# Forty columns for both score tiles, and another order of TensorE's work, in a two-layer recurrent attention kernel

## The chip, the core and the metric

The kernel runs on one core of a Trainium2 chip. The metric is the device time of one execution in microseconds. Before the change three runs gave 2647.1, 2651.34 and 2651.9 us; the median is 2651.34 us.

## What is computed

Two blocks, each applied twice with the same weights, with a residual around each. Block A is attention over segments of 32 rows with 8 memory rows; the output of the memory rows becomes the memory of the next segment, so the 64 segments are a recurrence. Block B is a gated feed-forward. All data are bf16.

```python
# x: (1, 2048, 576); 32 heads of 128; 8 memory rows; segments of 32 rows
def A(x, mem, Wq, Wk, Wv, Wo):
    for s in range(64):
        h = concat(mem, x[32*s : 32*s+32])          # 40 rows
        q, k, v = h @ Wq, h @ Wk, h @ Wv             # per head
        p = softmax(where(mask, q @ k.T * 128**-0.5, -1e9))   # 40 x 40 per head
        o = (p @ v) summed over heads through Wo
        mem = o[:8]; out.append(o[8:])
def B(x): return (silu(x @ w1) * (x @ w3)) @ w2      # 576 -> 4608 -> 576
x = x + A(layernorm(x)); x = x + B(layernorm(x))     # first layer
x = x + A(layernorm(x)); x = x + B(layernorm(x))     # second layer
```

## The kernel before

The second layer runs 8 steps behind the first (`LAG`), so there are 72 steps. Steps 0 to 7 and 64 to 71 hold one layer; the 56 steps between hold one segment of each layer, side by side: 80 columns move through the weights of Q and K, 40 for each layer.

The work is a list of nodes made by `make_nodes` (from line 263 on). A TensorE node is one letter of an order written out by hand as strings: `FIRST`, then `FOUR` eleven times, then `LAST` (`FOUR` covers four steps). TensorE issues strictly in this order. `plan` walks through it with a price and a due time for each node, and from that chooses the order on ACT, DVE, POOL and the DMA queues, and which of ACT and DVE evicts a bank. The letters that matter here:

- Q and q: the projection to queries and keys of four heads (eight in a one-layer step); Q takes the 512 rows of the model dimension that fill the array, q the 64 left over, for queries and keys in two row tiles at once.
- S: the scores of a group of eight heads (`scores`, called 4 times in a step). T: the transpose of the weights p on TensorE, in one-layer steps only; two-layer steps use a DMA transpose from `PB` to `PTS` on SP's queue, behind and ahead of the loads of feed-forward weights.
- P: p times values. O and o: the output projection and its tail. V, v, X, x, G, g: the value projections.
- F, f, W, w: the feed-forward up (F, its tail f) and down, with `W13`, its tail and `W2C` loaded from HBM into two buffers each.
- p, n, a, b: transposes around the residuals and layer norms.

Each node has a mode of the array: "full", "row" (two tiles of 64 rows), "col" (two tiles of 64 columns), "c32" (four of 32), or mixtures. Where a node can take either of two modes, `plan` gives it that of its neighbours.

In a two-layer step the queries of the two layers are two column tiles of the array. The weights loaded are the queries, the keys move. The tile of the first kind takes 64 columns (`R64`), of which the last 24 are columns that no later operation uses; the second takes `QW` = 40. Their outputs are rows 0 to 63 and 64 to 103 of one PSUM bank. The softmax (`sm_add` and what follows) then runs over rows 0 to 103, and `sm_pb` takes from it rows 0 to 39 and 64 to 103.

Every matmul is issued by one helper (line 729, `mm`), every activation by line 732, every DVE operation by line 735, every SP DMA by line 738, except the transposes (line 1274). The program is fully unrolled.

Of the kernel before, what the change touches and what calls it, by code (L numbers as in the profile page):

```python
# [13 lines left out]
P = 128  # L14
R64 = 64
# [6 lines left out]
QW = SEG + MEM  # L22
# [45 lines left out]
def role(t):  # L68

    return (t - LAG) % 2  # L70
# [156 lines left out]
def ewh(*ns):  # L227
# [2 lines left out]


FIRST = (
    "maqqQQQqSSvxVTXTqPQPSXSOOTPooOoTxPOoQqQSqqqSQQSSvTTVPTPOPoOTOPooOoQqqQvSSVqQQSqSTTPPOOoToTPaPOOooQqvqqSQVSQTQSqx"
    "PTSOPXOTToPoPOOooQqqpvSQVSnqQFFTSfqfPTQFOSPWTFOPoffTOPFOoooWQqfqQSFSVvqfqQQFTTSWPPFSOOxffXToFPWoTfOPFOooFQfqfqQS"
    "VqqvSQQSWTFSPTFfPOTOoPfWTOPFOoooFQffqqQSWQSqVvTSFfQqfWFSTafPFPOToWPTOPOOooobQqqqpQQQxSnXFvqfVSFfqqQQFfqSQPWQqfOS"
    "FPXxWOooPffFFPOOooWQQQqqfqFSFqfqQQQSFqqqfQQWFggfSGSGPGPgfFOOoPWGgfOPFOoooWFqqfQQFSqfqQQQSFvfqqQVSqWqQQfPPSFfOOWP"
    "FOfoFPaooOoWQQqqqqQSQQbSqqqQGSgQqPQGggSPGGPgOOOoPooOoQqqvpQpQQnSqqVqnSQFffqFQQPQqqfSFSOPWwfFOooFPfOWPwfFOooFqqfq"
    "QQQSqqqQQQSWwFfGSFqqfgQQPwWgSGFPGgfOOPWgfGFOoPOoooaqqQQQQqqwFfSSVvQQqqfFWSPwFqfqQQPFSwfOWOFPffFOwWoPOoooFfqqqQQW"
    "SQQqqqQSbQGSgqqQPQGSgOPGggOPGwOoPooOo"
)  # L240
FOUR = (
    "QqqqppQQvVSnnQFqfqqQQSFSFfqfqQQwWPFfPOOSWFoPowffFFPOOoowWQQfqfqFSFfqqqQQwQWSFgfqqQGQPQqgfSWSGFPOwoGggGPOPOOoooaF"
    "qfqqQQQSFqqqfQQQwWvSSVFPQFffqqQOPSWwoffFOPFOwPWOoooFqfqqQQWQSQqqqQQSwSbQQqgqgGSGPGPOoggGPOPOOooo"
)
LAST = (
    "QqqqppQQQqSvVSnnQQqqfFSqqQPQFSffOPFOwPWFOfFoPoofOoWQQQqqqwSQFQqqfGSqgQQPQqfSFGgqgPGSWwfFOFPOfgGOwoPOoooqqqQQQQqS"
    "WFfSVvqfqQFQQPWSwFqfqfQPFOSwWOPFffFOWwoPOoooFqqfqQQQSQFQqqfqQSVSvqqQQWwfSPFVvPWOwPOOobPooxOoXqpQpQqqvVSnSnQFFSTf"
    "fqPTQFSwFPWOTTffPOPOOooooFqffqQQSwFWSQvVqqQTSFPSTWPwFOTffTPOPOOoooowFWvxXVfqQQqfqSQSFFfqSQTwTSWPPFOffTOPFWTOFPwO"
    "ooooFfqfqQQSFSQwfqqQSWSVvTTFwWPffFPOTOTPWPOOoooowbqqpQQxvSSnXVFQfqqQTSTFfSPFPOwTOPFffooTOPFOoowQfqqqQSQSFvVTSQqf"
    "XPFSTwPOTffFPOTFPOOoooofxQfqqQSFSvVwTQqqFSffQwPTSFTPFPOffOTOPwOooooFQqQSqqvVSQQSqwTTSFPFPOoTOoTPffPOOoopfwfFFnFw"  # L250
    "fffFFFwffFFwfffFFwFwfffFFFwffFFwffFFwfffFFww"
)
ORDER = FIRST + FOUR * 11 + LAST
# [2 lines left out]
class Opt:  # L256

    qk, qkt, sc, tr, pv, wo, wog, vm = 0.0079, -0.0342, 0.0268, 0.1447, 0.0406, 0.2653, 0.0725, 0.1407
# [4 lines left out]
def make_nodes(em, nseg, pools, o=Opt, dma_bw=230e3, load_bw=380e3, tail_bw=330e3):  # L263
# [4 lines left out]
    def node(*a, **k):  # L268
        n = Node(*a, **k)
        n.prio += 1e-9 * len(nodes)  # L270
        nodes.append(n)
        return n

    def banks(n=2):
        return [Slot("bank") for _ in range(n)]
# [7 lines left out]
    def both(t):  # L283

        return len(layers_of(t - role(t))) == 2
# [104 lines left out]
    def step(t):  # L390
        ls = layers_of(t)
        nl = 2 if both(t) else 1
# [18 lines left out]
        for g, (h0, nh) in enumerate(GROUPS):  # L411
            qs, qe = [], []
            for uh, un in units(g, nl):
# [4 lines left out]
                if pre:  # L418
                    xl.append(node("DMA", 0.5, em.xq_load(t, uh, q), deps=[v[0] for v in [kept_qk.get((t // 4, uh // 4))] if v] + last_qk[-BACK:][:1], prio=pq - 0.3, acq=[q], lat=2.6, name="XL", ring=1.3))
                m_ = node("PE", 8 * un * mmq, em.qk(t, uh, un, b), deps=hx + hm[:1] + ([ld_h[g]] if t == 0 else []),  # L420
                          prio=pq, mode="full", acq=[q] + b, name="QK")
                last_qk.append(m_)
                n = node("PE", un * mmq, em.qk_tail(t, uh, un, b), deps=hx + hm + ([ld_h[g]] if t == 0 else []), prio=pq + o.qkt, mode="row",
                         acq=[q] + b, name="QKt")
                rd += [m_, n]
                me.setdefault(f"QK{g}", []).extend([m_, n])
                for r in (0, 1):
# [4 lines left out]
            s = banks(1)[0]  # L432
            sme = Slot("sme")
            pf = t + o.gstep * h0 / 8
            w40 = nh * QW
            sc = node("PE", nh * (0.0155 * nl if nl == 2 else 0.0255), em.scores(t, g, qs, s), deps=qe, prio=pf + o.sc, mode="col" if nl == 2 else "full/col",
                      acq=[s, sme], rel=[q for q, _, _ in qs], name="SC")
            a = node("DVE", dve(w40), em.sm_add(t, g, s, sme), deps=[sc], prio=pf, rel=[s], name="add")
            m_ = node("DVE", dve(w40, w40) + 0.13, em.sm_max(t, g, sme), deps=[a], prio=pf, name="maxsub")
# [14 lines left out]
            if paired(t):  # L454
                hn = [ht_ready[li, s] for s in (t + 1, t + 2) for li in (0, 1) if (li, s) in ht_ready]
                for blk in blks:
                    if blk // 2 not in vgs:
# [6 lines left out]
                      prio=pf + o.pv, mode="full/col", acq=b + ot, rel=[pts], name="PV")  # L464
# [21 lines left out]
        if nxt:  # L486
            m = 8 * len(nxt)
# [191 lines left out]
    for t in range(nst):  # L679
        if t % 4 == 2 and (t + 2) // 4 < ngrp:  # L680
            x_in((t + 2) // 4)
        if t == LAG:
            ht_mem[t].append(node("DVE", 0.1, em.init_mem(1, LAG), deps=[m0e] + reads_ht.get(LAG - R_HT, []), prio=LAG - 2, name="m0"))
        if role(t) == 0 or t == 0:
            vx_pair(t - role(t), t - 1 + o.vx)
        step(t)
        if t % 4 == 1 and t // 4 < ngrp:
            x_res(t // 4)
        if t % 4 == 3:
            job((t + 1) // 4 - 1)  # L690
        elif t == nst - 1:
            job(nst // 4)
# [12 lines left out]
class Emitter:  # L705
# [482 lines left out]
    def scores(self, t, g, qs, s):  # L1188

        def f(n):  # L1190
            nh = GROUPS[g][1]
            S = self.bk(s)[:, 0:nh * QW].rearrange("p (h k) -> p h k", h=nh)
            both = self.both(t)
            w = QW * self.nl(t)
            for i in range(max(un for _, _, un in qs)):
                for q, j0, un in qs:
                    if i >= un:
                        continue
                    Q = self.T.QKT[:, q.i]
                    for kd in ((0, 1) if both else (0,)):  # L1200
                        m = (R64 if kd == 0 else QW) if both else P if n.mode == "full" else QW
                        q0 = i * w + (QW * (kd ^ role(t)) if both else 0)
                        self.mm(S[64 * kd:64 * kd + m, j0 + i, :], Q[:, q0:q0 + m], Q[:, un * w + q0:un * w + q0 + QW],
                                True, True, **({"tile_position": (0, 64 * kd)} if n.mode == "col" else {}))
        return f
# [414 lines left out]
```

## Time and profile before

| | |
|---|---|
| median of 3 runs | 2651.34 us |
| span of the profiled execution | 2659.8 us (no time of its own beside the span is given) |
| TensorE: matmuls busy | 2571.8 us, 97% |
| TensorE: weight loads busy | 2214.4 us, 83% |
| DVE, ACT, POOL busy | 77%, 46%, 13% |
| `FIRST` | to 538.8 us |
| `FOUR`, eleven times | 538.8 to 2227.7 us |
| `LAST` | from 2227.7 us |

The profile is of one execution on the core. "PE" are matmuls, "PEld" weight loads, which overlap matmuls. A matmul's duration in the profile includes its way through the array; matmuls overlap, so what counts is the distance between starts. A row of the timeline gives start, length, engine, line, operation, tiles with shapes (the first shape of a merged group), and the count, with idle time ahead of it in brackets and what ended it. A row of waits gives who waited for whom: total us, times, longest. "issue" is idle time in which the engine waited for nothing that the profile shows.

### The profile page before, as it was taken

What the parts mean: (1) busy time and instruction counts of PE and PEld (TensorE: products, weight loads), DVE (VectorE), ACT (ScalarE), POOL (GpSimd) and SP (SyncE); (2) the same over time, 40 slices, a digit from 0 to 9 for tenths busy, and PEclk for the clock granted to TensorE, in tenths of its full rate; (3) what the DMA queues carried; (4) which work ended last, traced back from release to release, by engine and by line L of the source; (5) the groups of instructions that cost most, each with busy time, mean ns of one, the idle gap of its engine ahead of it and who ended that gap; (6) DMA issues with size and microseconds to landing.
All of it is one profiled execution on the core that took longest, in us unless ns stands there. A gap on an engine that the chain in (4) does not pass through costs nothing.

```text
span 2659.8 us, 132078 instructions
## 1 busy us (share of the span) xinstructions
PE 2571.8 (97%) x58776; PEld 2214.4 (83%) x58818; DVE 2045.3 (77%) x5137; ACT 1225.1 (46%) x3495; POOL 336.9 (13%) x399
## 2 busy tenths in 40 slices
PE   5899999999999999999999999999999999999998
PEld 4778887888888888888888888888888888888887
DVE  4777777777878778788777878877787788778876
ACT  2545453444545354454535444453544445344453
POOL 1111111011101111010111111011110111011110
PEclk8899999999999999999999999999999999999999
DMA  9045746565554655545465555546555554554457
GB/s 317 9 144 155 188 99 142 125 145 146 106 141 115 164 135 147 134 118 139 113 156 126 150 130 129 132 113 152 126 151 133 136 137 105 121 148 120 132 162 246
DMA packets 690428, 371.41 MB, mean 140 GB/s; under 512 B 234328, under 2 KB 682592, under 8 KB 689216
## 3 DMA queue, kind: packets, MB, share of 16 engines
q1 hardware_dynamic: 686320, 355.08, 52.6%
q8 instruction: 460, 7.54, 1.2%
q0 software_dynamic: 3024, 6.93, 1.0%
q10 hardware_dynamic: 512, 0.94, 0.1%
q14 instruction: 112, 0.92, 0.1%
HBM read 306.72 MB, written 2.36 MB: 116 GB/s over the span
## 4 chain that ended last, share of the span: by engine, by line
PE 85%; DMA 6%; DVE 5%; issue 1%; ACT 1%; SPq 0%; ACTq 0%; POOL 0%; DVEq 0%; POOLq 0%
PE bank L729 85%; DMA PTS<-PB 2%; DMA W<-in_B_w_dram 2%; DVE STAT L735 1%; DVE V L735 1%; DVE SME L735 1%; DVE PB L735 1%; DMA W<-in_A_Wq_dram 1%; DMA WO<-in_A_Wo_dram 0%; DMA W<-in_A_Wk_dram 0%; DVE HTT L735 0%; ACT V L732 0%; DVE XR L735 0%; DMA WV<-in_A_Wv_dram 0%; SPq L738 0%
## 5 line engine op out<-in xcount | busy, mean ns | idle before, releaser
L729 PEld LDWEIGHTS <-W 128*128 128x128 bf16 (+2 forms) x31872 | 1258.3, 100 | 150.0 <-issue 72.7
L729 PE MATMUL bank<-HT,W 128*128 128x80 bf16 (+3 forms) x23040 | 796.8, 197 | 23.6 <-issue 8.7
L729 PE MATMUL bank<-XTB,W 128*64 128x256 bf16 (+5 forms) x8832 | 667.4, 263 | 9.2 <-DMA W<-in_B_w_dram 5.8
L1264 POOL MEMSET PB<- 128x1024 bf16 x288 | 273.3, 953 | 1764.3 <-DMA PTS<-PB 1066.0
L732 ACT ACTIVATE QKT<-bank 128x128 bf16<-128x128 f32 (+2 forms) x1497 | 356.0, 316 | 276.9 <-PE bank L729 269.2
L729 PE MATMUL bank<-OT,WO 128*128 128x80 bf16 (+3 forms) x11520 | 414.3, 199 | 5.9 <-ACT OT L732 3.1
L729 PEld LDWEIGHTS <-WO 128*128 128x128 bf16 (+1 forms) x11520 | 385.9, 102 | 22.9 <-issue 10.8
L732 ACT ACTIVATE V<-bank 32x512 bf16<-32x512 f32 (+1 forms) x563 | 319.7, 585 | 174.5 <-PE bank L729 163.1
L729 PE MATMUL bank<-WV,HT 128*32 128x512 bf16 (+4 forms) x3735 | 366.0, 387 | 9.2 <-DMA WV<-in_A_Wv_dram 4.4
L729 PE MATMUL bank<-W2C,HTT 128*64 128x288 bf16 (+1 forms) x3136 | 317.2, 287 | 0.2 <-DMA W2C<-in_B_w_dram 0.2
L732 ACT ACTIVATE HTT<-bank 128x512 bf16<-128x512 f32 (+1 forms) x324 | 176.0, 550 | 277.9 <-PE bank L729 275.4
L735 DVE TENSOR_REDUCE STAT<-SME 104x8 f32<-104x320 f32 (+1 forms) x576 | 274.8, 477 | 29.9 <-ACT SME L732 20.3
L735 DVE TENSOR_TENSOR PB<-SME,STAT 40x128 bf16<-40x128 f32 (+4 forms) x912 | 275.3, 336 | 12.0 <-POOL PB L1264 1.0
L729 PEld LDWEIGHTS <-HT 128*32 128x32 bf16 (+5 forms) x3776 | 157.8, 101 | 139.6 <-issue 42.4
L735 DVE SCALAR_TENSOR_TENSOR HTT<-HTT,bank 128x512 bf16<-128x512 bf16 (+1 forms) x324 | 201.6, 622 | 82.3 <-ACT HTT L732 78.8
L732 ACT ACTIVATE SME<-SME 104x320 f32<-104x320 f32 (+1 forms) x288 | 135.5, 471 | 280.6 <-DVE SME L735 276.9
L729 PEld LDWEIGHTS <-HTT 128*64 128x64 bf16 (+1 forms) x3216 | 232.2, 105 | 32.6 <-issue 1.2
L735 DVE SCALAR_TENSOR_TENSOR XR<-bank,XR 128x288 f32<-128x288 f32 x574 | 240.6, 448 | 16.2 <-PE bank L729 11.8
L732 ACT ACTIVATE OT<-bank 128x320 bf16<-128x320 f32 (+2 forms) x430 | 164.1, 401 | 184.9 <-PE bank L729 171.9
L735 DVE CAST V<-bank 64x512 bf16<-64x512 f32 (+1 forms) x301 | 206.4, 686 | 43.4 <-PE bank L729 35.6
L735 DVE TENSOR_TENSOR HTT<-HTT,bank 128x512 bf16<-128x512 bf16 (+1 forms) x324 | 203.6, 628 | 28.1 <-PE bank L729 0.5
L735 DVE CAST QKT<-bank 128x192 bf16<-128x192 f32 (+4 forms) x423 | 124.4, 335 | 114.3 <-PE bank L729 111.3
(59 smaller groups left out, 1396.5 us busy)
## 6 DMA issues: line engine op xcount, KB each, us to landing
W<-in_B_w_dram SPq DMA_DIRECT2D x608, 256.0 KB, 3.7
W2C<-in_B_w_dram SPq DMA_DIRECT2D x304, 288.0 KB, 3.4
W<-in_B_w_dram SPq DMA_DIRECT2D x608, 32.0 KB, 3.3
W<-in_B_w_dram SPq DMA_DIRECT2D x16, 512.0 KB, 7.3
WO<-in_A_Wo_dram SPq DMA_DIRECT2D x4, 1152.0 KB, 9.8
XR<-in_A_x_dram POOLq DMA_DIRECT2D x16, 288.0 KB, 3.0
WV<-in_B_w_dram SPq DMA_DIRECT2D x8, 576.0 KB, 6.5
W<-in_A_Wq_dram SPq DMA_DIRECT2D x16, 256.0 KB, 7.1
```

The lines of the kernel that those rows point to most:

```text
L729: self.ch("PE", self.nc.tensor.matmul(out, lhsT=lhsT, rhs=rhs, start=start, stop=stop, skip_group_check=True, **k))
L732: self.ch("ACT", self.nc.scalar.activation(*a, **k))
L735: self.ch("DVE", getattr(self.nc.vector, fn_)(*a, **k))
L1264: return lambda n: self.ch("POOL", self.nc.gpsimd.memset(self.T.PB[:, pb.i, 0:GROUPS[g][1]], 0.0))
```

## The change

Three edits. In `scores` the first column tile loads `QW` = 40 columns too, so both tiles are alike. In `make_nodes` the price by which `plan` counts a score node of two layers falls from 0.0155 to 0.0126 us for each head and layer. And the three strings of the order are new: the same letters, each as often as before (709 in `FIRST`, 208 in `FOUR`, 604 in `LAST`), in another sequence, which was searched with a model of the instruction fetch for each 256 instructions.

```diff
 FIRST = (
-    "maqqQQQqSSvxVTXTqPQPSXSOOTPooOoTxPOoQqQSqqqSQQSSvTTVPTPOPoOTOPooOoQqqQvSSVqQQSqSTTPPOOoToTPaPOOooQqvqqSQVSQTQSqx"
...
+    "amqQqqSQQvSVTXxQSqTPPXTSPOoOOTPooOoQqQqvSSQqQSqSTxTVPTPOPTOPOOooooQqQSqVvSQqQQSTqPSTOPOTTPooPOOooaQqqqvSQVSqQTQST"
...
 FOUR = (
-    "QqqqppQQvVSnnQFqfqqQQSFSFfqfqQQwWPFfPOOSWFoPowffFFPOOoowWQQfqfqFSFfqqqQQwQWSFgfqqQGQPQqgfSWSGFPOwoGggGPOPOOoooaF"
-    "qfqqQQQSFqqqfQQQwWvSSVFPQFffqqQOPSWwoffFOPFOwPWOoooFqfqqQWQSQqqqQQSwSbQQqgqgGSGPGPOoggGPOPOOooo"
+    "QqqqppQQvVSnnQFqqfqQQSFSFfqfqQQPwFWPSffOFOwWoFffPFPOOoWoowQQqqqqQQFSSFqffqQQQQqfqgFSGWwPGSgfOPFGggoGPOPOOoowoFqq"
+    "fqQQWSQQQqqqfQwWSFSvVqfQPFOQqFSofPWwOPFffOFPWOowooFqqfqQQQSaWqqqQQQSwbSQQqgqGSGPgGPOggoGPOPOOooo"
 )
 LAST = (
-    "QqqqppQQQqSvVSnnQQqqfFSqqPQFSffOPFOwPWFOfFoPoofOoWQQQqqqwSQFQqqfGSqgQQPQqfSFGgqgPGSWwfFOFPOfgGOwoPOoooqqqQQQQqS"
...
+    "QQpqqqQQqSvpnSVqqQQnQqfSFfqFPQOSwPFfOWFPooFfPOOoowQfqqQQWQSqqfFSqqQQwWGSqgfFPQQqggGSOPGFPOgffoGFPOOoooWwqqQQQSFq"
...
-            sc = node("PE", nh * (0.0155 * nl if nl == 2 else 0.0255), em.scores(t, g, qs, s), deps=qe, prio=pf + o.sc, mode="col" if nl == 2 else "full/col",
+            sc = node("PE", nh * (0.0126 * nl if nl == 2 else 0.0255), em.scores(t, g, qs, s), deps=qe, prio=pf + o.sc, mode="col" if nl == 2 else "full/col",
...
-                        m = (R64 if kd == 0 else QW) if both else P if n.mode == "full" else QW
+                        m = P if n.mode == "full" and not both else QW
```

More of the change, by code (lines that the diff above doesn't have):

```diff
@@ L232 @@
 FIRST = (
-    "maqqQQQqSSvxVTXTqPQPSXSOOTPooOoTxPOoQqQSqqqSQQSSvTTVPTPOPoOTOPooOoQqqQvSSVqQQSqSTTPPOOoToTPaPOOooQqvqqSQVSQTQSqx"
[L234 to L237, printed above, removed]
@@ L238 @@
-    "QQQSqqqQQQSWwFfGSFqqfgQQPwWgSGFPGgfOOPWgfGFOoPOoooaqqQQQQqqwFfSSVvQQqqfFWSPwFqfqQQPFSwfOWOFPffFOwWoPOoooFfqqqQQW"
-    "SQQqqqQSbQGSgqqQPQGSgOPGggOPGwOoPooOo"
+    "amqQqqSQQvSVTXxQSqTPPXTSPOoOOTPooOoQqQqvSSQqQSqSTxTVPTPOPTOPOOooooQqQSqVvSQqQSTqPSTOPOTTPooPOOooaQqqqvSQVSqQTQST"
+    "PSPXOOToToPxPOOooQpVqqqvSQnQSFfQfqSTFPfTSOPFOoToWPfFTOPFOooWqfQQqqSvVSfFQQqfTSTFPSPXfOTOPooWFTxOPFOoofWqQFSvfqQV"
+    "SqfTQFQSTWPfqFOSPTFPOWOfoTooPFaOofFQfqWqSQfqQSFVSTvqfWQFfPTSFTOPoPWTOPOOooobQpQqqqQxSnQqqFQfSXFvVqfqQQSFWfqPQfxF"
@@ L240 @@
+    "SPOOXWPoFffOPFOoooWQQqfqqFSQQFQfqqQFSgfqGSFqfPQQqggGSWGPFOPOfgfGoOPFOoWooFQfqqQQSWfqqQFQSFqqfQVvSqqQFQWfSPPOOoaF"
+    "WfPFOPfooOoWQqqqqQQbSQQQqqSGSgqqQQGSgPGPOgGoPgOOPooOoQqqQppQQSvqqVnSnQFFfqQqfqQQfqSPFSFfPOWwOfFPoFwofWPOOooFfqqQ"
+    "QQqfqFSQwQWQSFfgqqGwQqSWQPFffgqFSGGPggGwOPOoaWPOOoooFfqqqQQQSvFQQqfqVSwQqWPQQSqqfFSFPfOwOoWFoffPFOwPWOooFfqqqQQQ"
+    "SWQqqqQQSwbqSQQgqgGSGPGPOggGPoOPOOooo"
 )
 FOUR = (
-    "QqqqppQQvVSnnQFqfqqQQSFSFfqfqQQwWPFfPOOSWFoPowffFFPOOoowWQQfqfqFSFfqqqQQwQWSFgfqqQGQPQqgfSWSGFPOwoGggGPOPOOoooaF"
@@ L243 @@
-    "qfqqQQQSFqqqfQQQwWvSSVFPQFffqqQOPSWwoffFOPFOwPWOoooFqfqqQQWQSQqqqQQSwSbQQqgqgGSGPGPOoggGPOPOOooo"
+    "QqqqppQQvVSnnQFqqfqQQSFSFfqfqQQPwFWPSffOFOwWoFffPFPOOoWoowQQqqqqQQFSSFqffqQQQQqfqgFSGWwPGSgfOPFGggoGPOPOOoowoFqq"
+    "fqQQWSQQQqqqfQwWSFSvVqfQPFOQqFSofPWwOPFffOFPWOowooFqqfqQQQSaWqqqQQQSwbSQQqgqGSGPgGPOggoGPOPOOooo"
 )
 LAST = (
-    "QqqqppQQQqSvVSnnQQqqfFSqqQPQFSffOPFOwPWFOfFoPoofOoWQQQqqqwSQFQqqfGSqgQQPQqfSFGgqgPGSWwfFOFPOfgGOwoPOoooqqqQQQQqS"
-    "WFfSVvqfqQFQQPWSwFqfqfQPFOSwWOPFffFOWwoPOoooFqqfqQQQSQFQqqfqQSVSvqqQQWwfSPFVvPWOwPOOobPooxOoXqpQpQqqvVSnSnQFFSTf"
@@ L248 @@
-    "fqPTQFSwFPWOTTffPOPOOooooFqffqQQSwFWSQvVqqQTSFPSTWPwFOTffTPOPOOoooowFWvxXVfqQQqfqSQSFFfqSQTwTSWPPFOffTOPFWTOFPwO"
-    "ooooFfqfqQQSFSQwfqqQSWSVvTTFwWPffFPOTOTPWPOOoooowbqqpQQxvSSnXVFQfqqQTSTFfSPFPOwTOPFffooTOPFOoowQfqqqQSQSFvVTSQqf"
-    "XPFSTwPOTffFPOTFPOOoooofxQfqqQSFSvVwTQqqFSffQwPTSFTPFPOffOTOPwOooooFQqQSqqvVSQQSqwTTSFPFPOoTOoTPffPOOoopfwfFFnFw"
+    "QQpqqqQQqSvpnSVqqQQnQqfSFfqFPQOSwPFfOWFPooFfPOOoowQfqqQQWQSqqfFSqqQQwWGSqgfFPQQqggGSOPGFPOgffoGFPOOoooWwqqQQQSFq"
+    "ffqFQQvSwWVqqFQQSqffqQPFPSWOwOfFooPfFwPOOoWoFqqfQQQqqSQQQSWFqqfqQQSvqfwSVFPVvOPWwPoOOPoboOxoXVqppQQSqqvQqnSnQSTF"
@@ L251 @@
+    "FPSTffOPFTOPfooOTwPWOooFfqqfQFwQSWSFQfqqVvTSQFWwPTSffFOFPwOTfTfPFPOOooooWxvVXqqQQSqfwQSWTSFQPqTffOPSFFOwoTWoTfPF"
+    "POOooFqffQFSQqqWSQwTSVvqffFQwWSPTFTPOPOoWoTwPOOoobQqqqpQSXvxQnSVSFfqTQPFOfTFTSPwPoOoffOTFPFOoowQfqVvfqSFQqfFQSwS"
+    "FQfTqFPTSwPOTOPXTOPfooOooxQqqvQSFSffqQVqSTFQFwTPSTPfOPofFFTOPOOooofwQqqQSvVSqQwQSqFSTTFPPOTOPTooffPOOoopwFffFnFw"
     "fffFFFwffFFwfffFFwFwfffFFFwffFFwffFFwfffFFww"
```

## The prediction

> **What bounds the kernel now.** I read the page first, then the waits of the matmul stream (PE) by stage, then the timeline around one score product, then the timeline of the weight loads (PEld) in a starved stretch.
>
> ```profile
> span 2659.8 us, 132078 instructions
> PE 2571.8 (97%) x58776; PEld 2214.4 (83%) x58818; DVE 2045.3 (77%) x5137; ACT 1225.1 (46%) x3495; POOL 336.9 (13%) x399
> PEclk8899999999999999999999999999999999999999
> PE 85%; DMA 6%; DVE 5%; issue 1%; ACT 1%; SPq 0%; ACTq 0%; POOL 0%; DVEq 0%; POOLq 0%
> q8 instruction: 460, 7.54, 1.2%
> ```
>
> TensorE is the bound: busy 97% of the span and 85% of the chain that ended last, at full clock but for the start. No other engine passes 77%. So the time moves with what TensorE issues, the changes of its array mode, and the holes in its stream. PE and PEld together hold 117,594 instructions; 460 instruction packets of 7.54 MB are 16.4 KB each, one per 256 of them.
>
> The holes, one answer for each stage: 140 to 300 us, 300 to 538.8 us, the eleven repeats of FOUR (538.8 to 2227.7 us), 2227.7 to 2535 us, and the end.
>
> ```profile
> PE bank L729 <- issue: 6.6, 8, 1.4
> ...
> PE bank L729 <- DMA PTS<-PB: 6.7, 4, 2.5
> ...
> PE bank L729 <- DMA W<-in_B_w_dram: 4.5, 7, 1.1
> PE bank L729 <- ACT HT L732: 3.8, 11, 0.3
> PE bank L729 <- issue: 3.3, 21, 0.2
> PE bank L729 <- DMA PTS<-PB: 2.8, 5, 1.3
> PE bank L729 <- ACT OT L732: 0.2, 1, 0.2
> ...
> PE bank L729 <- DMA PTS<-PB: 2.3, 2, 1.2
> ...
> PE bank L729 <- issue: 5.6, 7, 1.4
> ```
>
> Columns: total us, times, longest. The repeats are 1,688.9 us and hold 14.4 us of waits here; a new order can win little there. Before 300 and after 2535 us, where steps hold one layer, 12.2 us are "issue": nothing in the data was late.
>
> **Part 1: the score tile, 64 columns to 40.** One score product of a two-layer step is eight pairs of matmuls on two column tiles. The timeline around one, 1705.6 to 1707 us, and rows of the forms:
>
> ```profile
> 1705.42 0.60 PE L729 MATMUL bank<-HT,W 128*128 128x80 bf16 x12
> 1705.94 0.40 PE L729 MATMUL bank<-QKT 128*64 128x40 bf16 x15
> 1706.17 0.28 PE L729 MATMUL bank<-XTB,W 128*64 128x256 bf16 x1
> 1706.19 0.19 PE L729 MATMUL bank<-QKT 128*64 128x40 bf16 x1
> 1706.22 1.04 PE L729 MATMUL bank<-XTB,W 128*64 128x256 bf16 x15
> ...
> L729 PE MATMUL bank<-HT,W 128*128 128x80 bf16 x14336 | 560.8, 202 | 5.3 <-ACT HT L732 4.5 <-DVE HT L735 0.5 <-issue 0.4
> L729 PE MATMUL bank<-HT,W 64*128 64x40 bf16 x1024 | 21.1, 178 | 3.7 <-ACT HT L732 2.4 <-issue 1.2
> L729 PE MATMUL bank<-QKT 128*64 128x40 bf16 x1792 | 92.3, 188 | 0.0
> ```
>
> Fifteen of the sixteen matmuls have started when the feed-forward matmul of the 40-column tile starts at 1706.17. The 64-column tile starts its last score at 1706.19 and takes its own feed-forward matmul at 1706.22: it runs 0.05 us late. Both tiles then stream equal work and the mode change after them waits for the later, so those 0.05 us reach the end. With 40 columns in both, the late tile should finish with the early one. 1792 / 8 = 224 products x 0.05 = **-11.2 us**. Can both tiles be fed at the quick rate? The trace has no two 40-column tiles together, so the nearest row bounds it: the row tiles of a one-layer step, which also move 40 columns in two tiles:
>
> ```profile
> 187.27 0.36 PE L729 MATMUL bank<-HT,W 64*128 64x40 bf16 x16
> 186.17 1.04 PE L729 MATMUL bank<-HT,W 128*128 128x40 bf16 x35 [1.34 <-issue]
> ```
>
> (0.36 - 0.178) / 15 = 0.012 us between starts on two tiles, (1.04 - 0.18) / 34 = 0.025 on one: two tiles side by side keep 0.025 each, which is what the 40-column tile did above (eight in 0.23 us, with the start). So -11.2 is taken; the other end is 0 or slightly above, if the 40-column loads get in each other's way. A loss from the narrower tile itself is excluded: same number of instructions, fewer columns. Rows 40 to 63 of that score bank then hold old contents; the softmax still processes 104 rows, so DVE and ACT do the same work.
>
> The Trainium skill, "TensorE: Matmul & The Clock Gate", section "LDWEIGHTS (loading the stationary operand)", gives columns / 1.2 ns for a weight load. By it 24 columns less would be 20 ns a load, an estimated 0.16 us a product and 36 us in all, and the time 2616; the trace disagrees, since the two tiles end only 0.05 us apart.
>
> **Part 2: the order's mode changes.** Each letter of the order is one group of matmuls of one mode: whole array (Q, O), row tiles (q, f, g), column tiles (S of two layers, o, n, a, b), narrow column tiles (V, X), and either whole or column (P, F, G, W, w, p). A change of mode is paid whenever the next letter has no mode in common. Counted letter by letter, FOUR has 63 changes a repeat before and 66 after, FIRST 284 and 298, LAST 195 and 211: 1,172 and 1,235, so 63 more. The price is in the timeline above: twelve matmuls of 202 ns in 0.60 us, so starts (0.60 - 0.202) / 11 = 0.036 apart, the last at 1705.82, and the first score 0.12 later instead of 0.036. That is 0.085, and 0.01 of rounding on either side: 63 x 0.09 = **+5.7 us**, with 4.7 and 6.3 as the ends. No work hides it: TensorE itself is idle in it.
>
> **Part 3: blocks of 256 instructions.** The weight loads of the starved stretch, 184 to 192 us:
>
> ```profile
> 183.93 0.79 PEld L729 LDWEIGHTS <-W 128*128 128x128 bf16 x29
> 186.16 3.44 PEld L729 LDWEIGHTS <-W 128*128 128x128 bf16 x128 [1.44 <-issue]
> 190.72 0.43 PEld L729 LDWEIGHTS <-W 128*128 128x128 bf16 x11 [1.11 <-issue]
> ```
>
> Between two holes without a cause in the data lie exactly 128 weight loads, with their matmuls 256 instructions in 3.44 us. The next block was not there. These are the 12.2 us of "issue" from the first fence. With the spacings of Parts 1 and 2 I counted at how many places the next 256 instructions take under 3.44 us: FIRST 4,596 before, 3,935 after; LAST 2,406 and 1,649; in FOUR none in either (shortest 4.1 us). That is 20% fewer: 0.20 x 12.2 = **-2.5 us**. Ends: -12.2, if every boundary falls on a slow stretch, and +2.8, two more holes of 1.4 us, since where the boundaries fall is not in the strings.
>
> The Trainium skill, "Runtime: NRT & Kernel Launch", section "Instruction fetch mechanics", says that streaming in the 256-instruction blocks is mostly hidden. By it this term would be 0 and the time 2643; the trace disagrees at the one-layer ends, with holes of 1.44 and 1.11 us one block apart, and agrees in FOUR.
>
> **Part 4: data waits under the new order.** The late loads in FOUR, first and last of the five waits at one place (0.63, 0.46, 0.61, 0.38, 0.28), and one at another:
>
> ```profile
> 573.83 1.15 PE L729 MATMUL bank<-W2C,HTT 128*64 128x288 bf16 x15
> 574.91 2.90 PE L729 MATMUL bank<-XTB,W 64*128 64x256 bf16 x28
> 578.44 1.26 PE L729 MATMUL bank<-XTB,W 128*128 128x256 bf16 x10 [0.63 <-DMA W<-in_B_w_dram]
> ...
> 2113.77 0.94 PE L729 MATMUL bank<-XTB,W 128*128 128x256 bf16 x7 [0.28 <-DMA W<-in_B_w_dram]
> ...
> 1575.55 2.19 PE L729 MATMUL bank<-XTB,W 64*128 64x256 bf16 x19 [1.10 <-DMA W<-in_B_w_dram]
> ```
>
> The five belong to the letters "FoPowffFF": W13 has two buffers, so the last F needs the buffer that the first F gives back, and only about 4 us of work lie between. In the new FOUR the tightest such pair is "FqqfqQQSFSF", 5.4 us; the same letters, "FqfqqQQSFSF", lay 5.5 us apart before and never waited. So these 2.4 us go. The other 2.1 us of the 4.5 belong to the small tail load, which the f after next uses (5.8 us apart); the new order has pairs of 5.9 and 5.3, so they stay. Work between a score and its value product was at least 8.5 us in FOUR and becomes 9.6, but in FIRST it stays near 8, where the 6.7 us lie: PTS counted at 0. Sum **-2.4 us**; ends -16.3 (all of W 4.5 and PTS 6.7, 2.8, 2.3) and +11.8 (PTS waits doubled). The first Q after a step's last o keeps its place after "ooo" in FOUR, where ACT HT costs 0.34 eleven times. The planner's price of a score (0.0155 to 0.0126) orders only ACT, DVE, POOL and the queues; counted at nothing, because PE waits for DVE and ACT other than HT for 0.2 us in FOUR; if that cover goes it shows as more ACT or DVE rows, bounded with Part 4.
>
> **Sum.** -11.2 + 5.7 - 2.5 - 2.4 = -10.4 us. The profiled execution, 2659.8 us of span, ran 8.5 us above the median of the three runs; nothing else of it is given. Differences this small carry over unchanged: 2651.3 - 10.4 = **2641 us**.
>
> **Rivals.**
> (a) All holes go as well: fetch -12.2 and W -4.5 in place of -2.5 and -2.4, 2651.3 - 11.2 + 5.7 - 16.7 = 2629. For it: the holes stand one block apart, so an order that spaces dense letters can move them; against: 5,584 dense places remain.
> (b) Only Parts 1 and 2 hold and no hole shrinks: 2651.3 - 11.2 + 5.7 = 2646. For it: the order gains where boundaries happen to fall.
> (c) The narrower tile does nothing, because two 40-column loads and two matmuls in 25 ns are too many: +5.7 - 2.5 - 2.4, 2652. Against it: the row tiles' 0.012 us.
> (d) Slower: one PTS wait in each repeat. Transposes share SP's queue with loads that sit until TensorE frees their buffer:
>
> ```profile
> SPq L738 <- PE bank L729: 1169.1, 811, 77.7
> PTS<-PB SPq DMA_TRANSPOSE x224, 3.4
> ```
>
> A transpose behind such a load starts only when the buffer comes free, and its value product, with all of TensorE's stream behind it, waits. Waits for PTS reached 1.3 us in FOUR and 2.5 before it; at 1.9 in each of eleven repeats that is +20.9, so 2662. It makes the kernel slower by 0.2% from 1.43 us a repeat. Against it: the shortest distance in FOUR grows.
>
> **How the numbers follow.** 0.2% is 5.3 us, about what a measurement of this kernel can tell from no change: faster is under 2646.0, slower over 2656.6. Forecast 0.52, (a) 0.15, (b) 0.15, of which 0.03 falls just under the line, (c) 0.05, (d) 0.13. Faster 0.52 + 0.15 + 0.03 = 0.70, same 0.12 + 0.05 = 0.17, slower 0.13. The range runs from a little under (a), 2627, to 2657, where most of (d) begins; it leaves out some 0.07 of (a) and most of (d).
>
> **What would show it.** Part 1: score rows 128*40 only, and the feed-forward matmuls of both tiles starting within 0.01 us. Part 2: the same busy work with more short holes of PEld at mode changes. Part 3: "issue" in the first 300 and last 125 us, together near 10 us. Part 4: no W wait at the F place. A repeat should take about 152.8 instead of 153.5 us (1,688.9 / 11): -0.8 for 16 scores, +0.27 for three changes, -0.2 for the W waits. Wrong would be: both tiles spaced above 0.03 us, or a PTS, W or ACT wait that returns in every repeat.

## The result

| | before | changed kernel | ratio, 95% interval |
|---|---|---|---|
| first comparison, median | 2649.47 us (4 runs) | 2636.47 us (4 runs) | 0.995, 0.9936 to 0.9965 |
| second, another chip | 2659.36 us (17 runs) | 2639.64 us (5 runs) | 0.9936, 0.9924 to 0.9949 |

The kernel is faster, by 13 us in the first comparison and by 17 us by the ratio of the second; both intervals leave out 1. The forecast was 10.4 us less and 2641, the range 2627 to 2657.

The page of the changed kernel, the lines that answer to the first fence of the prediction:

```profile
span 2637.0 us, 132255 instructions
PE 2561.6 (97%) x58827; PEld 2182.7 (83%) x58855; DVE 2045.8 (78%) x5150; ACT 1227.2 (47%) x3482; POOL 337.8 (13%) x399
PEclk9999999999999999999999999999999999999999
PE 83%; DVE 9%; DMA 6%; issue 1%; ACT 1%; POOL 0%; SPq 0%; ACTq 0%; DVEq 0%; POOLq 0%
q8 instruction: 460, 7.54, 1.1%
```

TensorE still sets the time. The span fell by 22.8 us against the first profile of before, more than the runs did, because that profile was slow in its first stage. A second profile of before (2654.3 us) is the better measure. The stages by the windows view (from and to, length, then busy time and count of PE, PEld, DVE, ACT and POOL, the granted clock of TensorE, the DMA share and GB/s), cut where the first matmul of FOUR and of LAST stands: before (second profile), changed kernel.

```profile
0.00:529.70 529.70, 479.88 (x12381) 406.45 (x12382) 382.85 (x1009) 242.18 (x657) 75.28 (x97) 0.98 0.56 150
529.70:2221.60 1691.90, 1677.83 (x36458) 1450.11 (x36455) 1333.83 (x3300) 792.06 (x2365) 208.90 (x242) 1.00 0.55 134
2221.60:2654.30 432.70, 411.91 (x9990) 354.45 (x9987) 328.75 (x829) 190.43 (x474) 52.61 (x60) 0.99 0.55 149
```

```profile
0.00:528.10 528.10, 479.35 (x12424) 404.69 (x12429) 382.72 (x1004) 245.68 (x661) 75.82 (x97) 0.98 0.56 151
528.10:2210.40 1682.30, 1669.93 (x36350) 1423.62 (x36369) 1338.66 (x3333) 788.15 (x2332) 209.47 (x242) 1.00 0.57 135
2210.40:2637.00 426.60, 412.33 (x10065) 354.43 (x10063) 324.46 (x813) 193.40 (x489) 52.52 (x60) 0.99 0.55 151
```

FIRST 1.6 us less, the eleven repeats 9.6, LAST 6.1. (By this cut the first profile of before has 541.8, 1688.9 and 429.1; the marks in the prediction stand some 3 us early at both ends of FOUR, its length is the same.)

One score product in the changed kernel, timeline, and the form's row:

```profile
1703.91 1.94 PE L729 MATMUL bank<-XTB,W 128*64 128x256 bf16 x32
1705.68 0.36 PE L729 MATMUL bank<-QKT 128*40 128x40 bf16 x16
1705.89 0.31 PE L729 MATMUL bank<-OT,WO 128*64 128x80 bf16 x8
...
L729 PE MATMUL bank<-QKT 128*40 128x40 bf16 x3608 | 82.3, 181 | 0.0
```

All sixteen matmuls run as one group; the next node starts 0.21 us after the first score, on both tiles. Before, one tile started its next node after 0.23 us and the other after 0.28. The two 40-column tiles keep the rate that the row tiles showed.

The waits of TensorE by stage, changed kernel: 140 to 300 us, 300 us to the end of FIRST, FOUR, and from 2535 us (total, times, longest):

```profile
PE bank L729 <- issue: 4.2, 4, 2.1
...
PE bank L729 <- DMA W2C<-in_B_w_dram: 1.3, 1, 1.3
...
PE bank L729 <- DMA PTS<-PB: 0.7, 1, 0.7
...
PE bank L729 <- ACT HT L732: 3.8, 11, 0.3
PE bank L729 <- DMA PTS<-PB: 3.0, 6, 0.8
...
PE bank L729 <- DMA W2C<-in_B_w_dram: 1.2, 4, 0.5
...
PE bank L729 <- issue: 3.1, 3, 1.5
```

The W waits in FOUR (4.5 us) are gone, the holes called issue fell from 12.2 to 7.3 us, and the wait for PTS between 300 us and the end of FIRST fell from 6.7 to 0.7. In a second profile of the changed kernel these three are 0.4, 6.7 and 1.5 us. New in both are small waits for `W2C` in FOUR, 1.2 and 2.5 us (none and 0.5 before).

### The profile page after: what moved, and what is told of

Its sections match the earlier page's. It is cut to its first block, busy times and chain, and to the rows that moved or that the text cites. A ratio compares the mean times of both kernels' runs of the same rounds, so it can differ in the third digit from the quotient of the medians.

```text
span 2637.0 us, 132255 instructions
## 1 busy us (share of the span) xinstructions
PE 2561.6 (97%) x58827; PEld 2182.7 (83%) x58855; DVE 2045.8 (78%) x5150; ACT 1227.2 (47%) x3482; POOL 337.8 (13%) x399
## 4 chain that ended last, share of the span: by engine, by line
PE 83%; DVE 9%; DMA 6%; issue 1%; ACT 1%; POOL 0%; SPq 0%; ACTq 0%; DVEq 0%; POOLq 0%
PE bank L729 83%; DMA PTS<-PB 2%; DVE STAT L735 2%; DVE SME L735 2%; DMA W2C<-in_B_w_dram 1%; DVE PB L735 1%; DVE HTT L735 1%; DVE V L735 1%; DMA WV<-in_A_Wv_dram 1%; DMA W<-in_B_w_dram 1%; DVE XR L735 1%; DVE LNS L735 0%; DMA W<-in_A_Wq_dram 0%; DVE QKT L735 0%; ACT V L732 0%
## 5 line engine op out<-in xcount | busy, mean ns | idle before, releaser
L729 PEld LDWEIGHTS <-W 128*128 128x128 bf16 (+2 forms) x31760 | 1242.1, 100 | 131.5 <-issue 64.1
L732 ACT ACTIVATE QKT<-bank 128x256 bf16<-128x256 f32 (+2 forms) x1493 | 354.8, 318 | 314.0 <-PE bank L729 299.0
L732 ACT ACTIVATE V<-bank 32x512 bf16<-32x512 f32 (+1 forms) x572 | 326.2, 585 | 175.2 <-PE bank L729 162.7
L729 PEld LDWEIGHTS <-HT 128*32 128x32 bf16 (+4 forms) x3880 | 145.8, 101 | 141.0 <-issue 29.7
L735 DVE CAST V<-bank 64x512 bf16<-64x512 f32 (+1 forms) x292 | 200.1, 686 | 40.4 <-PE bank L729 34.6
L732 ACT ACTIVATE OT<-bank 128x320 bf16<-128x320 f32 (+2 forms) x400 | 154.4, 399 | 147.9 <-PE bank L729 135.3
L735 DVE CAST QKT<-bank 128x128 bf16<-128x128 f32 (+4 forms) x427 | 124.8, 333 | 102.3 <-PE bank L729 99.2
```

The source lines that it names most:

```text
L729: self.ch("PE", self.nc.tensor.matmul(out, lhsT=lhsT, rhs=rhs, start=start, stop=stop, skip_group_check=True, **k))
L732: self.ch("ACT", self.nc.scalar.activation(*a, **k))
L735: self.ch("DVE", getattr(self.nc.vector, fn_)(*a, **k))
```

## The experiments

**Columns or order.** The first run takes the old order and price and changes only the tile:

```diff
-                        m = (R64 if kd == 0 else QW) if both else P if n.mode == "full" else QW
+                        m = P if n.mode == "full" and not both else QW
```

> The old order and the old price, only the first score tile cut from 64 to 40 columns. My theory (the 64-column tile ends each score product 0.05 us late, and that reaches the end): 224 x 0.05 = 11.2 us less than before, about 2638; FOUR 0.8 us a repeat shorter, 128*40 score rows alone. Rival A (the narrower tile is covered or fed too slowly, the gain came from the order): within 3 us of before, about 2648. Rival B (the cheaper stream only moves the data waits): the score products shorten, but PTS or W waits grow by as much.

Measured: 0.9975 of before, 0.9961 to 0.9989: 6.7 us less (2.9 to 10.4). The second run is the opposite, the changed kernel with that line as it was; it holds the new price as well, which was not tried by itself.

> The new order and the new price, with the first score tile at 64 columns again. My theory: +5.7 us of mode changes against 2.5 us fewer fetch holes and 2.4 us fewer W waits, so about 1 us above before (2650), and some 11 us above the changed kernel. Rival A (the order is the gain): near 2637, as the changed kernel. Rival C (the fetch holes shrink by much more than I counted): 2640 to 2645.

Measured: 0.9975 as well, 0.9963 to 0.9987: 6.7 us less. So each half gives about half, and the sum, 13.4, is what the whole gave in the first comparison (17 in the second). My theory was wrong on the order, which was to cost 0.8; rival C of that run came nearest in time. Stages, first columns alone, then order alone:

```profile
0.00:529.80 529.80, 479.76 (x12379) 403.24 (x12380) 382.56 (x1008) 242.09 (x657) 75.19 (x97) 0.98 0.57 150
529.80:2212.60 1682.80, 1671.53 (x36460) 1423.00 (x36458) 1335.05 (x3300) 791.66 (x2366) 208.54 (x242) 1.00 0.56 135
2212.60:2640.00 427.40, 408.75 (x9990) 349.91 (x9986) 327.99 (x829) 190.48 (x473) 52.55 (x60) 1.00 0.55 151
```

```profile
0.00:526.30 526.30, 482.06 (x12427) 408.75 (x12428) 382.92 (x1004) 245.42 (x661) 75.74 (x97) 0.96 0.56 151
526.30:2218.20 1691.90, 1679.95 (x36371) 1445.49 (x36369) 1341.04 (x3333) 788.29 (x2333) 208.96 (x242) 1.00 0.56 134
2218.20:2645.10 426.90, 411.61 (x10067) 353.36 (x10063) 324.51 (x813) 193.26 (x489) 52.47 (x60) 1.00 0.56 151
```

FOUR falls with the columns (1691.9 to 1682.8) and not with the order (1691.9 in both).

One thing beside the data waits differs between these kernels. The mean granted clock of the timed runs was 0.9932 before, 0.9940 with the columns alone and 0.9951 with the order alone. If all of that difference fell on work, 0.0019 of 2650 us would be 5 us (an estimate); how much of it did is not known, so a part of the order's gain may have come by way of the clock.

**FOUR alone.** The changed kernel with the old string of FOUR.

```diff
 FOUR = (
-    "QqqqppQQvVSnnQFqqfqQQSFSFfqfqQQPwFWPSffOFOwWoFffPFPOOoWoowQQqqqq...
+    "QqqqppQQvVSnnQFqfqqQQSFSFfqfqQQwWPFfPOOSWFoPowffFFPOOoowWQQfqfqF...
```

> The changed kernel with FIRST and LAST new, but the old FOUR in the middle. My theory: FOUR has no fetch holes, so the new FOUR brings 0.22 us a repeat of W waits and costs 0.27 us of three mode changes: the same time as the changed kernel within 2 us; W waits of about 2.4 us in FOUR are back. Rival: the new FOUR carries the gain of the order; then this is 4 us or more slower than the changed kernel.

Measured: 0.9933 of before, 0.9917 to 0.9948; the changed kernel stands at 0.995 and 0.9936, so no difference shows. Its FOUR took 1683.2 us (1682.3 and 1684.5 in the two profiles of the changed kernel), and W waits of 5.9 us are back in it, longest 1.7. That agrees with three extra mode changes and the saved waits cancelling.

**Before once more.**

> The kernel before once more, for a second profile of it. The first profile had a span 10 us above the timed runs, with a lower clock in the first slices. My theory: this span is near 2648, FOUR again at 153.5 us a repeat, the issue holes at the same places of the instruction stream, and the difference lies in the first 540 us. Rival: the extra 10 us lie in FOUR, where data waits vary from run to run.

Measured: 2656.05 us, span 2654.3, with the stages shown above. FOUR takes 153.8 us a repeat against 153.5, FIRST 529.7 against 541.8: the slow part of the first profile was FIRST, as expected. The granted clock goes with it: 0.89 up to 140 us, 0.97 from there to 300 and 0.98 to 520 in the first profile, 0.91, 1.00 and 1.00 in the second. The run itself was not near 2648: on this chip before has a median of 2658.3 us (21 runs).

**FIRST and LAST.** The changed kernel again, and with one old string each.

> The changed kernel once more, timed on the same chip as the three below and against before. Expected as measured so far: 0.995 of before, PTS waits of about 1 us between 300 us and the end of FIRST, issue holes of 6 to 8 us in all.

Measured: 0.9936, as in the table of the result.

```diff
-FIRST = ("amqQqqSQQvSVTXxQSqTPPXTSPOoOOT...
+FIRST = ("maqqQQQqSSvxVTXTqPQPSXSOOTPooO...
```

> The changed kernel with the old FIRST; FOUR and LAST stay new, both score tiles 40 columns. My theory now: most of what the order gains is PTS waits in FIRST (6.7 to 7.0 us between 300 us and its end with the old string, 0.7 with the new), so these come back, and the time is 5 to 9 us above the changed kernel of this call. Rival A (the gain of the order is the fetch holes, in FIRST and LAST alike): 2 to 3 us above, PTS waits stay near 1. Rival B (FIRST gains nothing; the lower time came from LAST): the same time.

Measured: 0.9966, 0.9954 to 0.9978, median 10.0 us above the changed kernel on the same chip, a little over what was expected. Waits between 300 us and the end of FIRST, this kernel, then columns alone (old FIRST), then order alone (new FIRST):

```profile
PE bank L729 <- DMA PTS<-PB: 7.3, 4, 3.2
```

```profile
PE bank L729 <- DMA PTS<-PB: 7.0, 4, 2.8
```

```profile
PE bank L729 <- DMA PTS<-PB: 0.7, 1, 0.7
```

Whatever the width of the tile, the old FIRST waits about 7 us for PTS in this stretch (5.2 to 7.3 in six profiles) and the new one 0.7 to 1.9 in five. From 140 us to the end of FIRST the PTS waits are 9.4 us in this kernel and 2.5 in the changed kernel, 7 of the 9.9 us by which its FIRST is longer. One profile does not size the gain, though: the old FIRST took 529.7 to 541.8 us in six profiles, the new one 524.7 to 528.9.

```diff
-LAST = ("QQpqqqQQqSvpnSVqqQQnQqfSFfqFPQ...
+LAST = ("QqqqppQQQqSvVSnnQQqqfFSqqPQFSf...
```

> The changed kernel with the old LAST. My theory now: fetch holes at the end back to 4 to 6 us from 3, PTS waits after FOUR back to 2 or 3 us, against 16 mode changes less (1.4 us): 2 to 5 us above the changed kernel. Rival B (LAST carries the gain of the order): 6 us or more above. Rival C (LAST matters nothing): the same time.

Measured: 0.9975, 0.9963 to 0.9987, median 13.9 us above the changed kernel, 10 us by the ratios: more than expected, nearest to rival B. LAST took 434.4 us against 425.2 in the changed kernel, and the issue holes over 0.19 us add up to 9.9 us in the whole run against 7.1. Its longest wait between the end of FOUR and 2535 us:

```profile
PE bank L729 <- DVE XN L735: 3.9, 2, 3.6
```

One wait of 3.6 us, for `XN`, the input of a group of transposes, is the largest single part of the difference of 9.2 us; the holes of LAST are 6.5 us against 3.6. Columns alone, with the same old LAST, has 0.5 us of this wait and took 427.3 us for LAST, so the old LAST is not slow in this way each time. Old FIRST (+10), old LAST (+10 to 14) and old FOUR (0) add up to more than the order as a whole gives (7 to 10 us): the strings are not independent, and one reason may be that a string's number of instructions moves the ends of the 256-instruction blocks in the next. How the 10 to 14 us of LAST's twelve runs split between holes and waits stays open.

**Where a hole stands.** In `m0_tr`, ahead of the transposes of the memory, extra pairs of weight load and matmul, 64 in the kernel before:

```diff
+            for _ in range(64):
+                self.mm(self.bk(b)[:, 0:8], self.T.ident[:, 0:P], self.T.ident[:, 0:8], True, True)
             for c in range(5):
```

> The kernel before with 64 extra pairs of weight load and matmul (128 instructions, 8 columns each, into the bank of the first transposes) ahead of everything else, in time in which TensorE waits for its first input. My theory (a hole stands where a block of 256 instructions ends): every large issue hole stands at another place of the order, 64 pairs earlier in it, so that counted from the first instruction of the program all holes again lie at the same remainder of 256; their sum stays between 6 and 16 us. Rival (the holes belong to places of the order, such as a semaphore that the profile doesn't name): the same places and the same sum as before.

Measured: 2667.27 us in its one run (2656.17 to 2663.7 before, 17 runs). The holes over 0.19 us in the matmul stream add up to 19.8 us, against 12.8 and 10.5 in the two profiles of before: above the 16 that I gave as the upper end. Weight loads of the shifted kernel, 182 to 190 us:

```profile
182.94 0.44 PEld L729 LDWEIGHTS <-W 64*128 64x128 bf16 x24
185.32 1.90 PEld L729 LDWEIGHTS <-W 64*128 64x128 bf16 x74 [1.94 <-issue]
```

The hole that stood at 186.16 in the first profile, among loads of 128 rows, now stands among loads of 64. I counted the weight loads of the program up to the one behind each hole over 0.45 us and took the remainder by 128, one block (in order of time; the line divides the start of the program from its end):

```
before         86 86 86 84 83 | 47 45 44 44 44 44
shifted by 64  95 | 87 87 86 85 84 85 | 54 47 47 46 46 45 44 44 44
changed        89 85 | 49 47
changed again  89 87 85 | 50 49 48
```

In the first 300 us nearly all lie at 83 to 89, and near the end at 44 to 50, in both orders and with the shift. They belong to a count of instructions, not to a place of the order. (The remainder drifts slowly; other instructions of the stream, which are not counted, are a likely reason.)

**The changed kernel shifted.** The same lines in the changed kernel with 32, 64 and 96 pairs. In its order they come after the first transposes and are not free: the first projection starts 0.4, 1.3 and 1.9 us later.

> The changed kernel with 32 extra pairs (64 instructions) in front, which moves every end of a 256-instruction block by 64 instructions in the order. My theory: the issue holes change in place and in sum (5 to 7 us in the changed kernel, 3 to 15 here), all at the same remainder, and the time moves by the change of that sum, within 3 us. Rival (the holes are what the order makes them, wherever a block ends): sum and time as in the changed kernel.

> As the run with 32 pairs, with 64 (half a block). Theory and rival as there; one of the three shifts may lie below the changed kernel by up to 4 us, the sum that its holes still hold, and then beats both kernels.

> As the run with 32 pairs, with 96 (three quarters of a block). Theory and rival as there.

| extra pairs | ratio to before, 95% interval | median us | holes us |
|---|---|---|---|
| 32 | 0.9955, 0.9941 to 0.9970 | 2647.01 | 13.1 |
| 64 | 0.9944, 0.9926 to 0.9961 | 2644.27 | 9.3 |
| 96 | 0.9940, 0.9920 to 0.9959 | 2643.53 | 7.6 |

The sum of the holes changes with the shift alone and the medians follow in order, 3.5 us for 5.5 us of holes, though the intervals overlap. (The later start is not carried through whole: the first scores start at 19.98, 19.80 and 21.47 us, against 19.81 and 19.87 without the pairs.) The unshifted kernel, with 7.6 and 7.1 us of holes, already has a good alignment. None of the three is clearly below it.

**Which tile counts.** Before with both tiles at 64 columns; the extra outputs are not used.

```diff
-                        m = (R64 if kd == 0 else QW) if both else P if n.mode == "full" else QW
+                        m = R64 if both else P if n.mode == "full" else QW
```

> The kernel before with the second score tile widened too: 64 columns in both (the extra outputs are rows no later operation reads). My theory (the later of the two column tiles sets the end of a score product, so only its width counts): the same time as before within 3 us, FOUR without its waits at 152.7 us a repeat as before. Rival (each 64-column load costs on its own, and narrowing one tile gained half of what narrowing two would): 5 to 10 us above before, FOUR without waits at 153.1.

Measured: 0.9989, 0.9977 to 1.0001: not slower, the same within its measure. FOUR took 1687.6 us (1688.9 and 1691.9 before). The wider second tile costs nothing that shows: the later of the two sets the end. The rival's 5 to 10 us are excluded.

## Why the prediction came out right, and which steps did not

The sign and the size held, but two terms were wrong in opposite directions: the columns gave 6.7 us, not 11.2, and the order gained 6.7 us where I had it cost 0.8. That the sum came near is in this part luck.

**Part 1, -11.2.** The mechanism is shown: the late tile sets the end (both tiles at 64 columns cost nothing), and in FOUR the columns gave 9.1 us against the second profile of before and 6.1 against the first, where 176 products x 0.05 are 8.8. Data waits differ from profile to profile, so I take them off (all rows of the waits view but issue): FOUR less its data waits is 1677.7 to 1679.3 us in the four profiles with the old order and a 64-column tile, and 1672.2 in both with the old FOUR and two 40-column tiles. That is about 6 us, 0.03 to 0.04 a product. The step that failed is "those 0.05 us reach the end" for every product. Before (second profile) and columns alone, one place of the repeat with value projections behind the score, timelines:

```profile
1130.20 0.37 PE L729 MATMUL bank<-QKT 128*64 128x40 bf16 x15
1130.40 0.38 PE L729 MATMUL bank<-WV,HT 128*64 128x512 bf16 x1
...
1130.45 1.89 PE L729 MATMUL bank<-WV,HT 128*64 128x512 bf16 x15
...
1134.15 0.72 PE L729 MATMUL bank<-PTS,V 128*64 128x80 bf16 x16
1134.80 0.28 PE L729 MATMUL bank<-OT,WO 128*128 128x80 bf16 x3
```

```profile
1127.68 0.36 PE L729 MATMUL bank<-QKT 128*40 128x40 bf16 x16
1127.88 1.90 PE L729 MATMUL bank<-WV,HT 128*64 128x512 bf16 x16
...
1131.63 0.31 PE L729 MATMUL bank<-PTS,V 128*64 128x80 bf16 x8
1132.13 0.33 PE L729 MATMUL bank<-PTS,V 128*64 128x80 bf16 x8 [0.19 <-DVE V L735]
1132.39 0.28 PE L729 MATMUL bank<-OT,WO 128*128 128x80 bf16 x3
```

The score hands over both tiles 0.05 us earlier, and then P waits 0.19 us for DVE's eviction of V: from the score to O it is 4.60 us before and 4.71 with the narrow tile. This repeat is the worst of the eleven; in the ten others it is 4.48 before, and with the narrow tile 4.51 in nine and 4.59 in one, so the gain is gone here in each of them. A gain given to a stream with a wait close behind turns into that wait. I named such cover for the planner's price alone and did not ask it of the 0.05 us. This place is worth about 1 us in all (0.08 in each of eleven repeats, an estimate from these rows). How the rest of the missing 4.5 us splits between other places and the spread of the runs is not settled; the interval reaches 10.4.

The Trainium skill's figure for a weight load ("TensorE: Matmul & The Clock Gate", section "LDWEIGHTS (loading the stationary operand)") made 36 us of this term, an estimate; the whole change gave 13 to 17, and the tiles' distance of 0.05 us for eight loads, 6 ns a load, was the better measure.

**Part 2, +5.7.** Measured in FOUR alone, where 33 changes more were to cost 3.0 us. Order alone left FOUR at 1691.9 us; less its data waits that is 1680.4, against 1677.7 to 1679.3 with the old order. With two 40-column tiles the new FOUR has 1672.4 to 1674.6 in seven profiles and the old one 1672.2. So the new FOUR costs about 1 to 2 us beside its waits, and the saved W waits make up for it. For FIRST and LAST the term was not measured.

**Part 3, -2.5.** The cause was right, the size was not: the holes fell from 12.8 and 10.5 to 7.6 and 7.1 us, some 4.3. Dense places are not the measure; which of them a block's end meets is. One and the same order has 7.1 to 13.1 us of holes by a shift alone. I had written that the boundaries' places are not in the strings and still took the mean; the end of the range, -12.2, was honest about it. The Trainium skill's sentence that streaming in the blocks is mostly hidden ("Runtime: NRT & Kernel Launch", section "Instruction fetch mechanics") holds in FOUR, where the largest hole that the profiles list is 0.4 us, and not at the one-layer ends, where the shift alone moved the sum by 5 to 9 us.

**Part 4, -2.4.** The five W waits went as said. (The rows for FOUR in the first fence add up to 14.6 us of waits, not 14.4; nothing else rests on it.) The term that failed is "PTS counted at 0": in FIRST it was 6 us in the first two profiles. I took the work between S and P as the measure, which stayed near 8 us, and left out when SP's queue issues the transpose. Before, first profile, SP's issues and the wait that follows:

```profile
405.79 2.30 SPq L738 DMA_DIRECT2D W<-in_B_w_dram  x4
408.19 1.24 SPq L1274 DMA_TRANSPOSE PTS<-PB  x1
409.52 3.67 SPq L738 DMA_DIRECT2D W<-in_B_w_dram  x4
...
413.76 0.69 PE L729 MATMUL bank<-PTS,V 128*128 128x80 bf16 x8 [2.52 <-DMA PTS<-PB]
```

The transpose is issued behind four loads and ahead of four more, and P starts 5.6 us after its issue, where the median landing is 3.4. DVE's rows have its input `PB` written at 407.01, 1.2 us before the issue. This is the mechanism of rival (d), which I looked for in the new order as a loss. The old order has four such waits in this stretch; the other one that I looked at ends at 484.1 us, 4.3 us after an issue behind six loads and ahead of two. That the loads beside it delay the transpose is argued from these rows; it was not tried alone, and so the share of FIRST's gain that it made is open.

**Rivals.** (a), all holes gone, did not happen; under half of them went. (b) is refuted by the order's 6.7 us, (c) by the columns' 6.7 us, (d) by the PTS rows: 3.0 us in FOUR, longest 0.8.

## What to carry over

When a fully unrolled stream is the bound, count the holes that no data explain against the instruction count: they can belong to ends of fetch blocks, and then a few dummy instructions show it. Here they went with 8 us more in one run of before, as much as a real edit. Ask of every saved nanosecond what the next consumer waits for, since a gain in front of a near wait is not a gain; and look for a known bad wait in the kernel before as carefully as in the kernel after. Where two column tiles shared a node here, only the wider one counted.

## What was not expected of the hardware

Sixteen matmuls and sixteen weight loads of 40 columns in two column tiles go through in 0.20 to 0.22 us, 6 to 7 ns an instruction. And 128 instructions with no effect on the data, issued while TensorE had nothing else to do, went with 7 to 9 us more of holes (one profile against two).
